# Linear attention and a Mish feed-forward: the attention's small products in plain float32 on parts of TensorE's array

## The chip, the core and the metric

The kernel runs on one core of one Trainium2 chip. The metric is the device time of one execution in microseconds. A token here is one row of the output; the core has TensorE (PE), VectorE (DVE), ScalarE (ACT), GpSimd (POOL) and the queue of SyncE (SP), from which most transfers are started.

## What is computed

```python
kv  = einsum('bhsd,bhse->bhde', k, v)        # 8 batches, 8 heads, 576 rows, 64 columns
out = einsum('bhsd,bhde->bhse', q, kv)
rms = sqrt(mean(out * out, axis=-1) + 1e-6)
x   = (out / rms * g_norm), heads side by side  # 4608 tokens x 512
h   = x @ w_in                                # 512 x 2048
g   = h * tanh(softplus(h))                   # Mish
y   = g @ w_out                               # 2048 x 512, float32
```

The attention has no softmax, so k^T v is a 64 x 64 matrix for each head, and it is small beside the two dense products.

## The kernel before

The 4608 tokens are nine token tiles of 512 (`T`), numbered j = 0 to 8. A batch has 576 rows, so most token tiles hold two segments, the end of batch j - 1 and the beginning of batch j (`segments(j)`): 64 and 448 columns in tile 1, 128 and 384 in tile 2, and so on to 512 alone in tile 8.

**The dense products.** Float32 operands are split into a high part (`nc.scalar.copy` into float32r, line 122) and the rest (`nc.vector.tensor_sub`, line 123). A product is then three float32r matmuls: low times high, high times low, high times high. Both dense products also use a seven-product form of the 2 x 2 block product (forms named A11, S1 and so on, made by `x_form` for the first dense product). One such product is a *slot*: twelve matmuls of 128 x 128 by 256 columns in `mm_in` (line 536). Each token tile has 28 slots (`NS`), so tile j's own products run in slots 28 j to 28 j + 27. The output stage (`mm_out`, line 790) runs after all nine tiles.

**What sets the order.** The order of every engine is written out by hand: `at(slot, f)` puts work behind the product of a slot, `then` puts an eviction ahead of it. Engines and queues take their instructions in that order. The attention of tile j runs in the 28 slots of tile j - 1, and the products k^T v of batch b in those of tile b - 2.

**The attention of a token tile** is done in two units u of four heads, that is, two head pairs a. The steps of a unit, by name:

- `load`, `transpose`: q comes in and is transposed (on DVE from tile 2 on, line 339; on TensorE in tiles 0 and 1).
- `halves`: from tile 2 (`T32`) on, q is split into two float32r parts (lines 122 and 123, tiles fl, fh, fa).
- `project`: x = kv^T q for each head pair and segment. The two 64 x 64 matrices of a pair lie on the diagonal of a 128 x 128 matrix of which the rest is zero. Tiles 0 and 1 use plain float32 (line 369), the others three float32r matmuls (lines 372 to 374).
- `square`, `scaled`: ACT squares the result, DVE scales it by g into the tile x of the dense product.
- `squares`: from tile 2 on, the squares are split as q is.
- `sums`: the squares of each head are added up by a matmul with a 128 x 8 matrix of ones and zeros (`sel`), all eight heads into the same eight partitions of one bank, lines 408 (float32) and 410, 411 (float32r).
- `rstd`, `keep`, `spread`, `normalize`: ACT makes the reciprocal roots, SP stores them to a DRAM tile (line 426) and loads them back on all partitions (line 433), and DVE multiplies x by them (line 441).

**k^T v** of a batch is made in four parts of one head pair each (`k_load`, `k_product`, line 261): four blocks of 128 rows and one of 64, in plain float32, with the even head in PSUM partitions 0 to 63 and the odd head in 64 to 127. Batch 0 has a form of its own on two diagonal 64 x 64 tiles (`kv_first_product`, line 243), which writes the same PSUM bank. `kv_keep` copies the result, splits it (line 285) and places it on the diagonal. The staging tiles of k and v have two buffers.

Of the kernel before, what the change touches and what calls it, by code (L numbers as in the profile page):

```python
# [8 lines left out]
F32 = mybir.dt.float32  # L9
# [18 lines left out]
def linear_attention_rms_mish_ffn(  # L28
# [82 lines left out]
    sel = const.tile([P, NKC, H], F32R, name="sel")  # L111
# [9 lines left out]
    def split(hi, lo, src):  # L121
        nc.scalar.copy(hi, src)  # L122
        nc.vector.tensor_sub(lo, src, hi.bitcast(F32))  # L123
# [102 lines left out]

    kv0 = []

    def kv_first(n):
# [22 lines left out]
    def kv_product(b, h0, nh, km, kr, vm, vr):  # L254
        for i in range(nh // 2):
            for c in range(CM + 1):
                for o in range(2):
                    h = 2 * i + o
                    d = slice(c * D, (c + 1) * D)
                    kt, vt = (km[:, h, d], vm[:, h, d]) if c < CM else (kr[:, h, :], vr[:, h, :])  # L260
                    nc.tensor.matmul(kvps[o * D:(o + 1) * D, b % 2, h0 // 2 + i, :], kt, vt, start=(c == 0), stop=(c == CM))  # L261

    kvf, kvt = [], []

    def kv_tiles():
        for n in range(T32):
            kvf.append(pools["kvf"].tile([P, NKC, P], F32, name=f"kvf{n}"))
            nc.gpsimd.memset(kvf[n], 0.0)  # L270
        for n in range(2):
            kvt.append(kvs.tile([P, 2, NKC, P], F32R, name=f"kv{n}"))
            nc.gpsimd.memset(kvt[n].bitcast(F32), 0.0)

    def kv_keep(b, n):
        for r in (slice(0, D), slice(D, P)):
            if b < T32:
                nc.scalar.copy(kvf[b][r, n, r], kvps[r, b % 2, n, :])
        if b < T32 - 1:
            return  # L280
        t = kvt[b % 2]
        for r in (slice(0, D), slice(D, P)):
            nc.scalar.copy(t[r, 0, n, r], kvps[r, b % 2, n, :])
        for r in (slice(0, D), slice(D, P)):
            nc.vector.tensor_sub(t[r, 1, n, r], kvps[r, b % 2, n, :], t[r, 0, n, r].bitcast(F32))


    def segments(j):
# [18 lines left out]
    qs, ss = {}, {}  # L307

    def unit_steps(j, u):
        st = {}  # L310

        def load():


            t = qs[u] = att.tile([P, 2, T // R * D], F32, name="qs")
            for i in (0, 2, 1, 3):
                for b, s0, cols in segments(j):
                    run = (cols.stop - cols.start) // R * D
                    src = q[b, 4 * u + i // 2, s0:s0 + 1, R * (i % 2):]
                    src = bass.AP(src.tensor, src.offset, [[run, R], [2 * S * D, 2], [1, run - R]])  # L320
# [25 lines left out]
            else:  # L346
                nc.scalar.copy(t, st["ps"])

        def parts(t):
            hi = att.tile([P, 2, T], F32R, name="fh")  # L350
            lo = att.tile([P, 2, T], F32R, name="fa")
            split(hi, lo, t)
            return hi, lo

        def halves():
            if j >= T32:
                st["qh"], st["ql"] = parts(st["q"])

        def project():
            if j == 0 and u == 1:  # L360
                st["x"] = [bank_new("bc").rearrange("p m t -> p (m t)") for _ in range(2)]
            else:
                x2 = st["x2"] = ps_t.tile([P, 2, T], F32, name="x2")
                st["x"] = [x2[:, a] for a in range(2)]
            for a in range(2):
                ps, hp = st["x"][a], 2 * u + a
                for b, _, c in segments(j):
                    if j < T32:
                        nc.tensor.matmul(ps[:, c], kvf[b][:, hp, :], st["q"][:, a, c], start=True, stop=True)
                        continue  # L370
                    kh, kl, qh, ql = kvt[b % 2][:, 0, hp, :], kvt[b % 2][:, 1, hp, :], st["qh"][:, a, c], st["ql"][:, a, c]
                    nc.tensor.matmul(ps[:, c], kl, qh, start=True, stop=False)  # L372
                    nc.tensor.matmul(ps[:, c], kh, ql, start=False, stop=False)  # L373
                    nc.tensor.matmul(ps[:, c], kh, qh, start=False, stop=True)  # L374

        def square():
            st["s"] = att.tile([P, 2, T], F32, name="fl" if j >= T32 else "fh" if j == 0 and u else "fa")
            if "x2" in st:
                nc.scalar.square(st["s"], st["x2"])
            else:  # L380
                for a in range(2):
                    nc.scalar.square(st["s"][:, a], st["x"][a])
# [5 lines left out]
            else:  # L388
                nc.vector.tensor_scalar(o, st["x2"], gcol, None, ALU.mult)

        def squares():
            if j >= T32:
                st["sh"], st["sl"] = parts(st["s"])

        def sums():
            if j == 0:
                st["ss"] = []
                for a in range(2):
                    ps = bank_new("a").rearrange("p m t -> p (m t)") if u == 0 else ps_t.tile([P, T], F32, name="ss") if a == 0 else kvps.rearrange("p b n d -> p (b n d)")
                    nc.tensor.matmul(ps, ones, st["s"][:, a], start=True, stop=True)  # L400
                    st["ss"].append(ps)
                return
            if u == 0:
                ss[j] = ps_t.tile([H, T], F32, name="ss")
            for a in range(2):
                e = sel[:, 2 * u + a, :]
                if j < T32:
                    nc.tensor.matmul(ss[j], e.bitcast(F32), st["s"][:, a], start=u == a == 0, stop=u == a == 1)
                else:
                    nc.tensor.matmul(ss[j], e, st["sl"][:, a], start=u == a == 0, stop=False)  # L410
                    nc.tensor.matmul(ss[j], e, st["sh"][:, a], start=False, stop=u == a == 1)

        def rstd():
            if j == 0:
                r = st["r"] = st["s"]
                for a in range(2):
                    nc.scalar.activation(r[:, a], st["ss"][a], AF.Ln, bias=eps, scale=1.0 / D)
                nc.scalar.activation(r, r, AF.Exp, scale=-0.5)
                return
            r = st["r"] = att.tile([H, T], F32, name="fa" if j < T32 else "fl")  # L420
            nc.scalar.preload_act_table_set("natural_log_exp_and_others")  # L421
            nc.scalar.activation(r, ss[j], AF.Ln, bias=eps[0:H], scale=1.0 / D)
            nc.scalar.activation(r, r, AF.Exp, scale=-0.5)

        def keep():
            nc.sync.dma_start(rd[j], st["r"])

        def spread():

# [10 lines left out]
            else:  # L440
                nc.vector.tensor_mul(o, o, st["rr"])

        return {f.__name__: f for f in (load, transpose, turned, halves, project, square, scaled, squares, sums, rstd, keep, spread, normalize)}


    x = fp.tile([P, NKC, T], F32, name="gf")
# [122 lines left out]
        for s in steps:  # L569
            units[j][u][s]()  # L570

    open_pools(wst, ("w64", 1), ("wd", 1), ("kvf", 1))

    def w64_room():
        return pools["w64"].tile([P, 4, 2 * P, 2], U32, name="w64")
# [35 lines left out]
    weights(2, LOAD)  # L611
    weights(3, LOAD)
    make_identity(nc, ident)
    kv_tiles()
# [4 lines left out]
    nc.gpsimd.memset(sel.bitcast(F32), 0.0)  # L619
    for hp in range(NKC):  # L620
        for o in range(2):
            nc.gpsimd.memset(sel[o * D:(o + 1) * D, hp, 2 * hp + o:2 * hp + o + 1].bitcast(F32), 1.0)

    weights(0, SCALE, JOIN, DIFF)
    do(0, 0, "transpose", "turned")
# [40 lines left out]
    at(5, lambda: kv_keep(1, slice(0, NKC)))  # L666
    for b in range(2, B):
        t = NS * (b - 2)
        loads = (5, 6, 14, 16) if b == 2 else (20 - NS, 22 - NS, 4, 6) if b == 3 else (8 - NS, 10 - NS, 4, 6)
        for p in range(4):  # L670
            at(t + loads[p], lambda b=b, p=p: k_load(b, p))
            at(t + ((12, 14, 16, 18) if b == 2 else (2, 4, 6, 8))[p], lambda b=b, p=p: k_product(b, p))
        at(t + (20 if b == 2 else 11), lambda b=b: kv_keep(b, slice(0, NKC)))

    def attention(j):

        def spread():
# [3 lines left out]
        t = NS * (j - 1)  # L681
        steps = (
            (0, 2, "transpose"), (0, 3, "turned"), (0, 6, "project", "square", "scaled"), (1, 8, "transpose"),
            (1, 9, "turned"), (0, 9, "sums"), (1, 11, "project", "square", "scaled"), (1, 15, "sums"),
        ) if j == 1 else (
            (0, 8 - NS if j > 2 else 9 - NS, "load"), (0, 20 - NS, "transpose"), (1, 22 - NS, "load"), (0, 25 - NS, "halves"),
            (0, 0, "project"), (0, 3, "square", "scaled"), (0, 4, "squares"), (1, 5, "transpose"), (0, 6, "sums"),
            (1, 8, "halves"), (1, 10, "project"), (1, 12, "square", "scaled"), (1, 13, "squares"), (1, 15, "sums"),
        )
        for u, n, *names in steps + ((1, 16, "rstd"), (1, 18, "keep"), (0, 19, "spread0"), (0, 23, "normalize"), (1, 24, "normalize")):  # L690
            at(t + n, lambda u=u, names=names: do(j, u, *names))
# [304 lines left out]
```

## Time and profile before

| what | value |
|---|---|
| median of 3 runs | 871.11 us (870.78 to 873.40) |
| profiled execution: span from first to last instruction | 867.2 us |
| granted TensorE clock, mean | 0.990 |
| TensorE busy | 829.2 us, 96% of the span |
| DVE busy | 604.5 us, 70% |
| ACT busy | 462.4 us, 53% |
| POOL busy | 102.5 us, 12% |
| HBM traffic | 106.89 MB read, 56.49 MB written |

The profile is of one execution. Its page gives the span, and no time for what lies around it, so the span stands beside the runs: these are 3.6 to 6.2 us longer. Lines such as L261 are lines of the kernel file before. "PE" is matmul work and "PEld" the loading of stationary operands. Matmuls are pipelined, so the records of neighbours overlap: what a group costs is read from the start of its first record to the start of the next group. A plain float32 matmul of the program stands as two records. Names in `out<-in` are the program's tiles without buffer numbers: `x` is the projection's PSUM tile, `s` that of k^T v, `a` and `bc` the PSUM banks of the dense product, `gf` its operands' forms, `ss` the sums.

### The profile page before, as it was taken

Reading aid. Unit: us, or ns where it says so; the run is one execution under the profiler, and the core shown is the slowest. Engines: PE = TensorE matmul, PEld = TensorE weight load, DVE = VectorE, ACT = ScalarE, POOL = GpSimd, SP = SyncE. Lnnn points to the kernel's source line nnn. Section 1 sums busy time; section 2 is a strip of 40 time slices with the busy share of each in tenths; the row PEclk is TensorE's granted clock in tenths of the full one; section 3 lists DMA queues with packets and bytes.
Section 4 is the critical chain, followed back from the end, with each engine's and each line's share of the span. In section 5 each row is a group of like instructions: output and inputs, shape, how many; then the busy total and the mean of one; then the engine's idle time right before and its main releaser. Section 6 shows DMA issues by size and latency. Waiting matters only on the chain.

```text
span 867.2 us, 17267 instructions
## 1 busy us (share of the span) xinstructions
PE 829.2 (96%) x7036; PEld 799.0 (92%) x7036; DVE 604.5 (70%) x778; ACT 462.4 (53%) x681; POOL 102.5 (12%) x173
## 2 busy tenths in 40 slices
PE   4868999999999999999999999999999999999997
PEld 3656999999999999999899999999999999999997
DVE  4788676757766576677765788767767777776772
ACT  3666656655566656566666654444443344334441
POOL 2000122232222313112122100000000000000000
PEclk9889999999999999999999999999999999999999
DMA  9975686878877674757376972543444444344421
GB/s 277 258 230 150 202 261 229 282 240 276 249 234 224 217 228 168 239 182 271 128 233 239 383 260 78 179 145 114 134 131 122 122 122 122 122 125 147 148 69 49
DMA packets 121007, 164.52 MB, mean 190 GB/s; under 512 B 25184, under 2 KB 96096, under 8 KB 120672
## 3 DMA queue, kind: packets, MB, share of 16 engines
q1 hardware_dynamic: 107328, 116.42, 44.5%
q0 software_dynamic: 13504, 46.93, 14.4%
q8 instruction: 55, 0.90, 0.5%
q14 instruction: 24, 0.20, 0.1%
q10 hardware_dynamic: 96, 0.07, 0.0%
HBM read 106.89 MB, written 56.49 MB: 188 GB/s over the span
## 4 chain that ended last, share of the span: by engine, by line
PE 76%; ACT 9%; DVE 8%; issue 3%; DMA 2%; SPq 2%; ACTq 0%; DVEq 0%
PE a L790 22%; PE a L536 18%; PE bc L790 16%; PE bc L536 14%; PE s L261 2%; DVE gf L123 1%; ACT wf L122 1%; ACT gf L122 1%; SPq L304 1%; PE x L373 1%; ACT L421 1%; PE x L374 1%; DVE ur L557 1%; PE x L372 1%; DVE wf L123 1%
## 5 line engine op out<-in xcount | busy, mean ns | idle before, releaser
L790 PE MATMUL a<-wf,gf 128*128 128x256 f32 x1632 | 201.8, 283 | 0.5 <-DVE ur L835 0.5
L790 PEld LDWEIGHTS a<-wf,gf 128*128 128x128 f32 x1632 | 198.4, 192 | 0.7 <-DVE ur L835 0.7
L123 DVE TENSOR_TENSOR gf<-g,gf 128x1024 fp32r<-128x1024 f32 (+1 forms) x123 | 132.9, 1087 | 87.1 <-ACT gf L122 87.1
L536 PE MATMUL a<-gf,wf 128*128 128x256 f32 x1296 | 172.5, 286 | 6.9 <-ACT ur L513 6.6
L536 PE MATMUL bc<-gf,wf 128*128 128x256 f32 x1296 | 172.5, 286 | 2.1 <-ACT gf L122 1.9
L536 PEld LDWEIGHTS a<-gf,wf 128*128 128x128 f32 x1296 | 162.7, 192 | 12.3 <-ACT ur L513 8.3
L536 PEld LDWEIGHTS bc<-gf,wf 128*128 128x128 f32 x1296 | 163.3, 193 | 3.7 <-ACT gf L122 2.0
L122 ACT CAST gf<-g 128x1024 fp32r<-128x1024 f32 (+1 forms) x123 | 114.6, 939 | 90.7 <-DVE g L770 65.7
L790 PE MATMUL bc<-wf,gf 128*128 128x256 f32 x1224 | 152.7, 283 | 0.9 <-DVE gf L123 0.9
L790 PEld LDWEIGHTS bc<-wf,gf 128*128 128x128 f32 x1224 | 149.4, 192 | 1.3 <-ACT gf L122 0.7
L119 ACT ACTIVATE ur<-ur 128x1024 f32<-128x1024 f32 x36 | 38.1, 1059 | 54.7 <-DVE ur L557 54.7
L536 PE MATMUL a<-a,wf 128*128 128x256 f32 x432 | 58.8, 286 | 5.2 <-DVE ur L557 5.2
L536 PEld LDWEIGHTS a<-a,wf 128*128 128x128 f32 x432 | 55.1, 192 | 8.2 <-DVE ur L557 6.6
L123 DVE TENSOR_TENSOR fa<-fl,fh 128x1024 fp32r<-128x1024 f32 x28 | 34.2, 1221 | 18.1 <-ACT fh L122 16.9
L122 ACT CAST gf<-a 128x1024 fp32r<-128x1024 f32 x17 | 17.9, 1051 | 53.4 <-DVE a L767 50.9
L123 DVE TENSOR_TENSOR gf<-gf 128x512 fp32r<-128x512 f32 x45 | 30.2, 690 | 23.1 <-ACT gf L122 23.1
L513 ACT COPY ur<-a 128x512 f32<-128x512 f32 (+1 forms) x53 | 27.4, 517 | 32.2 <-PE a L790 24.6
L560 POOL DMA_DIRECT2D gd<-ula x36 | 26.1, 725 | 146.3 <-ACT ula L119 104.6
L122 ACT CAST gf<-gf 128x512 fp32r<-128x512 f32 x45 | 26.9, 618 | 30.1 <-DVE gf L460 17.5
L557 DVE TENSOR_TENSOR ula<-bc,ula 128x512 f32<-128x512 f32 x36 | 24.7, 686 | 23.8 <-PE bc L536 23.6
L504 ACT COPY ur<-bc 128x512 f32<-128x512 f32 (+1 forms) x53 | 27.5, 518 | 24.5 <-PE bc L790 23.0
L555 POOL DMA_DIRECT2D gd<-ulb x36 | 25.6, 711 | 94.7 <-ACT ulb L119 87.7
(147 smaller groups left out, 944.8 us busy)
## 6 DMA issues: line engine op xcount, KB each, us to landing
g<-gd SPq DMA_DIRECT2D x18, 2048.0 KB, 8.6
gd<-ur POOLq DMA_DIRECT2D x36, 512.0 KB, 5.1
gd<-ula POOLq DMA_DIRECT2D x36, 256.0 KB, 4.4
gd<-ulb POOLq DMA_DIRECT2D x36, 256.0 KB, 4.8
w<-in_moe_w_out_dram SPq DMA_DIRECT2D x32, 256.0 KB, 5.3
km<-in_k_dram SPq DMA_DIRECT2D x28, 256.0 KB, 4.4
vm<-in_v_dram SPq DMA_DIRECT2D x28, 256.0 KB, 4.9
wf<-wod SPq DMA_DIRECT2D x6, 896.0 KB, 8.0
```

The costliest lines, as they stand in the source:

```text
L119: nc.scalar.activation(o, i, AF.Mish)
L122: nc.scalar.copy(hi, src)
L123: nc.vector.tensor_sub(lo, src, hi.bitcast(F32))
L261: nc.tensor.matmul(kvps[o * D:(o + 1) * D, b % 2, h0 // 2 + i, :], kt, vt, start=(c == 0), stop=(c == CM))
L304: nc.sync.dma_start(rows[j][t0 - c * P:t1 - c * P, c, h0 * D:(h0 + n) * D].rearrange("p (h d) -> p h d", d=D), src)
L504: then(t + 2, lambda: nc.scalar.copy(dst(st, "22"), st["c"]))
L513: then(t + 4, lambda: nc.scalar.copy(dst(st, "12"), st["a"]))
L536: nc.tensor.matmul(bank[:, jj], w[:, right, a, kc, :], xf[:, b, kc, :], start=first and jj == kc == s == 0, stop=(kc == 1 and s == 2), ski ...
L555: at(t + 2, lambda: eng.dma_start(left[:, :, TH:T], o))
L557: nc.vector.tensor_add(o, bank, o)
L560: at(t + 3, lambda: eng.dma_start(left[:, :, 0:TH], o))
L790: nc.tensor.matmul(bank, gf[:, a, c, :], wo[c][:, :, right, b, :], start=first and c == s == 0, stop=(c == NF2 - 1 and s == 2), skip_group ...
```

## The change

All of the attention's products are plain float32 now, and each is placed on a part of the array.

- `halves`, `squares` and the split of k^T v are gone, and with them the zero-filled matrices. `kv_keep` copies a batch's matrices once, as they lie in PSUM.
- `project` issues a 64 x 64 matmul for each head of a pair instead of a 128 x 128 one for the pair. From tile 2 on, the second pair of a unit is *turned*: its q comes in with the heads exchanged, k^T v with its halves exchanged, so the four heads of a unit use four different 64 x 64 tiles of the array. Tiles 0 and 1 aren't turned, so both pairs use the two diagonal tiles. Batch 1 is needed both ways, so DVE also copies it exchanged (`kvx`).
- `sums` is done once for a tile from tile 1 on, in slot 15, as four 128 x 32 products: head pair hp goes to the column strip of partitions 32 hp to 32 hp + 31. `keep` stores two rows of each strip, four transfers instead of one.
- The plan of k^T v moves: two parts go behind the same slot, from batch 3 on two in slot 0 and two in slot 10, where the projections also are, and their loads go out earlier relative to them.

```diff
+    def half(o, turned=False):
+        o = 1 - o if turned else o
+        return slice(o * D, (o + 1) * D)
...
-                    nc.tensor.matmul(kvps[o * D:(o + 1) * D, b % 2, h0 // 2 + i, :], kt, vt, start=(c == 0), stop=(c == CM))
+                    hp = h0 // 2 + i
+                    nc.tensor.matmul(kvps[half(o, b >= T32 and hp % 2), b % 2, hp, :], kt, vt, start=(c == 0), stop=(c == CM))
...
+    kvt = [kvs.tile([P, NKC, D], F32, name=f"kv{n}") for n in range(2)]
+    kvx = kvs.tile([P, 2, D], F32, name="kvx")
     def kv_keep(b, n):
...
+        nc.scalar.copy(kvt[b % 2][:, n], kvps[:, b % 2, n, :])
+        if b == T32 - 1:
+            for o in range(2):
+                nc.vector.tensor_copy(kvx[half(o, True)], kvps[half(o), b % 2, 1::2, :])
...
-        def halves():
-            if j >= T32:
-                st["qh"], st["ql"] = parts(st["q"])
...
-            for a in range(2):
-                ps, hp = st["x"][a], 2 * u + a
-                for b, _, c in segments(j):
...
-                    nc.tensor.matmul(ps[:, c], kl, qh, start=True, stop=False)
-                    nc.tensor.matmul(ps[:, c], kh, ql, start=False, stop=False)
-                    nc.tensor.matmul(ps[:, c], kh, qh, start=False, stop=True)
+            for b, _, c in segments(j):
+                for a in range(2):
+                    hp, turned = 2 * u + a, j >= T32 and a == 1
+                    kv = kvx[:, u] if turned and b < T32 else kvt[b % 2][:, hp]
+                    for o in range(2):
+                        r = half(o, turned)
+                        nc.tensor.matmul(st["x"][a][half(o), c], kv[r], st["q"][r, a, c], start=True, stop=True)
...
-                    nc.tensor.matmul(ss[j], e, st["sl"][:, a], start=u == a == 0, stop=False)
-                    nc.tensor.matmul(ss[j], e, st["sh"][:, a], start=False, stop=u == a == 1)
+            ss[j] = ps_t.tile([P, T], F32, name="ss")
+            for n in range(2):
+                for a in range(2):
+                    hp = 2 * n + a
+                    nc.tensor.matmul(ss[j][hp * R:(hp + 1) * R], sel, sq[j, n][:, a], start=True, stop=True)
...
-            nc.sync.dma_start(rd[j], st["r"])
+            for n in range(NKC):
+                nc.sync.dma_start(rd[j][2 * n:2 * n + 2], st["r"][n * R:n * R + 2])
...
-        loads = (5, 6, 14, 16) if b == 2 else (20 - NS, 22 - NS, 4, 6) if b == 3 else (8 - NS, 10 - NS, 4, 6)
+        loads = (5, 6, 14, 15) if b == 2 else (19 - NS, 20 - NS, 1, 2) if b == 3 else (11 - NS, 12 - NS, 1, 2)
...
-            at(t + ((12, 14, 16, 18) if b == 2 else (2, 4, 6, 8))[p], lambda b=b, p=p: k_product(b, p))
+            at(t + ((12, 13, 18, 18) if b == 2 else (0, 0, 10, 10))[p], lambda b=b, p=p: k_product(b, p))
```

How the order moves on TensorE, at the beginning of the slots in which tile 4's attention runs. The names with a number are single buffers: `x2` is the projection's PSUM tile, `kv0` and `kv1` the kept k^T v of two batches, `s2` the PSUM tile of k^T v. Before, from the second half of the first projection on:

```order
L372 MATMUL x2_2435<-fh_2379,kv1_175 128x256
L373 MATMUL x2_2435<-fa_2380,kv1_175 128x256
L374 MATMUL x2_2435<-fh_2379,kv1_175 128x256
L372 MATMUL x2_2435<-fh_2379,kv0_173 128x256
L373 MATMUL x2_2435<-fa_2380,kv0_173 128x256
L374 MATMUL x2_2435<-fh_2379,kv0_173 128x256
L536 MATMUL bc_2451<-gf_342,wf0_210 128x256 x6
L536 MATMUL bc_2451<-gf_342,wf1_281 128x256 x6
L536 MATMUL a_2287<-a22_482,wf6_764 128x256 x6
L536 MATMUL a_2287<-a22_482,wf7_850 128x256 x6
L261 MATMUL s2_123<-vm_2022,km_2020 64x64 x8
L261 MATMUL s2_123<-vr_2023,kr_2021 64x64 x2
```

The same place now:

```order
L510 MATMUL a<-gf,wf_196 128x256 x6
L510 MATMUL a<-gf,wf_268 128x256 x6
L267 MATMUL s_123<-vm,km 64x64 x8
L267 MATMUL s_123<-vr,kr 64x64 x2
L267 MATMUL s_123<-vm,km 64x64 x8
L267 MATMUL s_123<-vr,kr 64x64 x2
L354 MATMUL x_2387<-fl,kv_125 64x256 x4
L354 MATMUL x_2387<-fl,kv_124 64x256 x4
L510 MATMUL bc<-gf,wf_196 128x256 x6
```

Two k^T v products that stood two slots apart stand together ahead of the projection, and the projection's twelve matmuls became eight.

On SP's queue, around the store of tile 3's reciprocal roots, before (`rd3` is the DRAM tile, `qs` the next q, `w64` a block of w_out):

```order
L322 DMA qs_2032<-in_q_dram 32x2x480 x8
L138 DMA w64_2044<-in_moe_w_out_dram 128x2x256 x2
L222 DMA km_2076<-in_k_dram 128x2x256
L223 DMA kr_2077<-in_k_dram 64x2x64
L222 DMA vm_2078<-in_v_dram 128x2x256
L223 DMA vr_2079<-in_v_dram 64x2x64
L426 DMA rd3_115<-fl_2211 8x512
L433 DMA fh_2258<-rd3_115 64x2x512 x2
L433 DMA fa_2261<-rd3_115 64x2x512 x2
```

and now:

```order
L315 DMA qs_1947<-in_q_dram 32x2x480 x8
L138 DMA w64_1959<-in_moe_w_out_dram 128x2x256 x2
L222 DMA km_2036<-in_k_dram 128x2x256
L223 DMA kr_2037<-in_k_dram 64x2x64
L222 DMA vm_2038<-in_v_dram 128x2x256
L223 DMA vr_2039<-in_v_dram 64x2x64
L222 DMA km_2057<-in_k_dram 128x2x256
L223 DMA kr_2058<-in_k_dram 64x2x64
L222 DMA vm_2059<-in_v_dram 128x2x256
L223 DMA vr_2060<-in_v_dram 64x2x64
L400 DMA rd3_115<-fl_2144 2x512 x4
L407 DMA fh_2194<-rd3_115 64x2x512 x2
```

The store became four transfers, and both loads for the next batch's first two products stand ahead of it.

More of the change, by code (lines that the diff above doesn't have):

```diff
@@ L110, in linear_attention_rms_mish_ffn @@
     ones = const.tile([P, P], F32, name="ones")
-    sel = const.tile([P, NKC, H], F32R, name="sel")
+    sel = const.tile([P, R], F32, name="sel")
     gd = [tc.dram_tile([P, NFC, T], F32, name=f"gd{i}") for i in range(NT)]
@@ L306, in linear_attention_rms_mish_ffn @@
     rows = {}
-    qs, ss = {}, {}
+    qs, ss, sq = {}, {}, {}
     def unit_steps(j, u):
@@ L441, in normalize @@
                 nc.vector.tensor_mul(o, o, st["rr"])
-        return {f.__name__: f for f in (load, transpose, turned, halves, project, square, scaled, squares, sums, rstd, keep, spread, normalize)}
+        return {f.__name__: f for f in (load, transpose, turned, project, square, scaled, sums, rstd, keep, spread, normalize)}
     x = fp.tile([P, NKC, T], F32, name="gf")
@@ L618, in linear_attention_rms_mish_ffn @@
     nc.gpsimd.memset(ones[D:P, D:P], 1.0)
[L619 to L622, printed above, removed]
+    nc.gpsimd.memset(sel, 0.0)
+    for o in range(2):
+        nc.gpsimd.memset(sel[o * D:(o + 1) * D, o:o + 1], 1.0)
     weights(0, SCALE, JOIN, DIFF)
```

57 lines of the change are left out of this document (10 added, 47 removed).

## The prediction

> **What bounds the kernel now.** I read the page's engine shares first, then busy time by stretch, then what TensorE waits for in the long middle stretch, then TensorE's own timeline in one token tile.
>
> ```profile
> PE 829.2 (96%) x7036; PEld 799.0 (92%) x7036; DVE 604.5 (70%) x778; ACT 462.4 (53%) x681; POOL 102.5 (12%) x173
> ```
>
> ```profile
> 0.00:40.00 40.00, 24.90 (x241) 17.68 (x242) 22.80 (x31) 20.84 (x31) 5.98 (x25) 0.94 1.01 282
> 40.00:100.00 60.00, 48.86 (x396) 41.37 (x397) 49.84 (x71) 40.08 (x58) 4.77 (x7) 0.93 0.56 169
> 100.00:440.00 340.00, 336.32 (x2935) 321.94 (x2933) 235.36 (x344) 212.50 (x320) 78.45 (x121) 1.00 0.71 228
> ```
>
> The columns are PE, weight loads, DVE, ACT, POOL, granted clock, DMA share and GB/s. From 100 to 440 us TensorE is busy for 336.3 of 340 us at the full clock, while DVE is busy for 235 and ACT for 213. There, what TensorE is spared comes off the end, and what DVE and ACT are spared does not. Before 100 us TensorE has gaps. The output stage after 440 us is untouched.
>
> ```profile
> PE a L536 <- DVE ur L557: 3.5, 2, 1.8
> PE a L536 <- ACT ur L513: 3.3, 2, 3.2
> ```
>
> ```profile
> L536 PE MATMUL a<-gf,wf 128*128 128x256 f32 x984 | 129.2, 284 | 2.6 <-ACT ur L513 2.6
> L410 PE MATMUL ss<-fa,sel 128*8 128x512 f32 x28 | 11.1, 396 | 1.0 <-DVE fa L123 1.0
> ```
>
> The first two rows are TensorE's largest waits from 40 to 100 us. The other two are groups from 100 to 440, with the idle time ahead of them as the last figure: 2.6 us for an eviction by ACT, and 1.0 us for the split of the squares.
>
> TensorE's timeline in token tile 4:
>
> ```profile
> 210.53 0.28 PE L372 MATMUL x<-fh,kv 128*128 128x256 f32 x1
> ...
> 211.97 1.60 PE L536 MATMUL bc<-gf,wf 128*128 128x256 f32 x12
> 213.41 1.60 PE L536 MATMUL a<-a,wf 128*128 128x256 f32 x12
> 214.94 0.69 PE L261 MATMUL s<-vm,km 128*64 128x64 f32 x16
> 215.55 0.33 PE L261 MATMUL s<-vr,kr 64*64 64x64 f32 x4
> 215.81 1.69 PE L536 MATMUL a<-gf,wf 128*128 128x256 f32 x12
> 217.34 1.60 PE L536 MATMUL bc<-gf,wf 128*128 128x256 f32 x12
> ...
> 222.80 0.69 PE L261 MATMUL s<-vm,km 128*64 128x64 f32 x16
> 223.42 0.33 PE L261 MATMUL s<-vr,kr 64*64 64x64 f32 x4
> 223.68 0.40 PE L410 MATMUL ss<-fa,sel 128*8 128x512 f32 x1
> ...
> 224.62 0.65 PE L536 MATMUL a<-gf,wf 128*128 128x256 f32 x4
> ```
>
> I take differences of starts, since ends overlap. A slot's twelve products take 1.44 us (211.97 to 213.41). A projection takes 1.44. A k^T v product takes 0.87, but the slots on both sides of it take 1.53, so it costs 0.87 + 2 x 0.09 = 1.05. The sums take 0.94 behind a product whose leaving price they contain, so I count 0.9.
>
> **Two prices that the change rests on.** First, plain float32 on one tile, and what it costs to enter and leave it:
>
> ```profile
> 69.57 1.88 PE L408 MATMUL ss<-fa,sel 128*8 128x512 f32 x4
> 71.38 1.69 PE L536 MATMUL a<-gf,wf 128*128 128x256 f32 x12
> 72.91 1.60 PE L536 MATMUL bc<-gf,wf 128*128 128x256 f32 x12
> ```
>
> ```profile
> L408 PE MATMUL ss<-fa,sel 128*8 128x512 f32 x8 | 3.8, 593 | 0.0
> ```
>
> Line 408 issues two products of 512 columns, and four records stand there: float32 runs as two passes. Their pitch is (1.88 - 0.59) / 3 = 0.43 us, or 54 ns for 64 columns. The block takes 69.57 to 71.38, 1.81 us; the slot behind it is 0.09 too long, and I add as much ahead. That makes 1.99 = 4 x 0.43 + 0.27, so 0.27 is what such a block pays beside its passes.
>
> Second, tiles at once. The product rows above hold 16 passes of 64 columns in two column tiles: 16 x 54 ns is 0.86 us in a row, and they take 0.61. Four more passes take 0.26 with all entering and leaving. The first batch uses two diagonal tiles, which write the same PSUM bank:
>
> ```profile
> 21.51 2.31 PE L243 MATMUL s<-wf,wf 64*64 64x64 f32 x72 [0.60 <-DMA wf<-in_v_dram]
> ```
>
> 72 passes in a row would be 3.9 us; 2.31 / 72 is 32 ns a pass, tail included, so two tiles work at once. The trace has pairs by columns and pairs on the diagonal; four at once, two row halves writing the same PSUM partitions (in other banks), and four column strips it has not. For a projection of 512 columns the bounds are therefore two passes' time (0.86 us, four at once) and eight (3.44, one at once), with two at once at 1.72. I take 0.86 for both: the four projection tiles ask of each row half what the two column tiles of L261 do, two streams. The strips are less sure, with four streams on all rows.
>
> The Trainium skill, TensorEngine Tiling (Array Packing), under Gotcha 1: PSUM Pressure, says that different row tiles cannot access one PSUM bank at the same time. By that rule a projection's two tiles of one head pair, which write one bank, could not overlap. The diagonal row above disagrees: both its tiles write one bank, and a pass takes 32 ns rather than 54.
>
> **The change part by part.**
>
> *Token tiles 2 to 6 (five).* Now each has four products, two projections and two sums: 4 x 1.05 + 2 x 1.6 + 2 x 0.9 = 9.2 us. The 1.6 is the middle of the split projections' range, by these rows (448 + 64 columns: 1.81; one segment: 1.39):
>
> ```profile
> 358.90 0.37 PE L372 MATMUL x<-fh,kv 128*128 128x448 f32 x1
> ...
> 360.71 1.56 PE L536 MATMUL bc<-gf,wf 128*128 128x256 f32 x11
> ...
> 406.58 0.40 PE L372 MATMUL x<-fh,kv 128*128 128x512 f32 x1
> ...
> 407.97 1.60 PE L536 MATMUL bc<-gf,wf 128*128 128x256 f32 x12
> ```
>
> Then, there are two float32 blocks of two products and a projection: 2 x (0.61 + 0.26) + 0.86 + 0.1 for the change of tile shape + 0.18 for entering and leaving = 2.9; and one block of sums, 0.86 + 0.27 = 1.13. That is 6.9, say 7.0. Saved: 2.2 x 5 = 11.0 us.
>
> *Tiles 7 and 8* have no products left. Tile 7: 2 x 1.81 + 1.8 + half of the 1.0 us wait for the split, 5.9, becomes 3 x 1.13 = 3.4: saved 2.5. Tile 8: 2 x 1.39 + 1.8 + 0.5 = 5.1 becomes 3.4: saved 1.7.
>
> *Tile 1* already uses float32. Its projections aren't turned, so both head pairs lie on the same two tiles: four pass times, as now, nothing saved. Its two sums blocks, 4.0 us, become one of 1.13: 2.85 on TensorE, but in the stretch with gaps. The bounds are 0 and 2.85; I take the middle, 1.5. Tile 0's projections also remain four pass times: 0. Two products of the second batch share a block: 0.2.
>
> *DVE and ACT.*
>
> ```profile
> L123 DVE TENSOR_TENSOR fa<-fl,fh 128x1024 fp32r<-128x1024 f32 x28 | 34.2, 1221 | 18.1 <-ACT fh L122 16.9
> L122 ACT CAST fh<-fl 128x1024 fp32r<-128x1024 f32 x28 | 29.4, 1051 | 0.0
> ```
>
> These 56 instructions go, 34 us of DVE and 29 of ACT, beside smaller copies of k^T v. They lie under TensorE's work and are worth only what shortens its 2.6 us of waiting for ACT: 0 to 2.6, and I take 0.6, since an eviction also waits for its own product. The reciprocal roots run on 128 partitions instead of 8, with the same 512 elements in each: 0.
>
> *SP.* One store of the roots becomes four.
>
> ```profile
> L426 SPq DMA_DIRECT2D rd<-fl x7: 281/311/316, 144.5 to 438.4; - x7
> ...
> DVE gf L441 <- DMA fa<-rd: 11.7, 8, 2.2
> ...
> PE x L334 <- DMA wf<-in_q_dram: 7.0, 1, 7.0
> ```
>
> Three more issues of 0.31 us make the spread 0.9 us later, and DVE's normalize already waits for it. Behind it on DVE stand the input forms of the next tile, due four to five slots later (1.44 us each), and a split of 1.2 us no longer stands between them. Bounds 0 and 8 x 0.9 = 7.5; I take 0. The q loads keep their count. The k and v loads go out eight or nine slots ahead of their second products, where now they go two ahead: no DMA wait appears. POOL loses memsets at the start, when TensorE waits for q anyway: 0.
>
> Sum: 11.0 + 2.5 + 1.7 + 1.5 + 0.2 + 0.6 = 17.5 us. The profiled span of 867.2 becomes 849.7. The runs are 3.6 to 6.2 us above that span, and nothing here touches this rest, so the median goes from 871.1 to 853.6.
>
> **The rivals.**
> 1. *Strips go two at a time.* Eight sums blocks (tiles 1 to 8) cost 0.86 more each: 6.9, so 860.5. For it: no row has four streams over all rows. Against: two streams show no loss.
> 2. *The projection goes two at a time* because row halves that share output partitions queue: 14 x 0.86 = 12.0, so 865.6; with rival 1 too, 872.5, no change. For it: no row of such a pair. Against: diagonal and column pairs overlap fully.
> 3. *Slower: TensorE starts a tile's second pass before it looks at the next tile.* Four tiles then take five pass times instead of two, 3 x 0.43 more for each of the 8 sums blocks, and 4.5 in a projection of two half segments, 1.1 more for each of 14: 25.7, so 879.3. It decides above 0.86 + 17.5 / 22 = 1.66 us a block. Against: four passes of 64 columns (215.55) leave after 0.26, and the 72 keep 32 ns.
> 4. *The bank rule holds* though L243 speaks against it: a projection goes two at a time (12.0), and tiles 0 and 1 lose their pairs, 4 x 1.72 = 6.9: 872.5. The page is the one named above.
> 5. *New waits give back half*: blocks of 2.9 us pile evictions, or the later spread stalls the next tile: 4 to 8 us, so about 860.
>
> **How the numbers follow.** All four at once, 853.6 with its own range 849 to 858: 0.60. Rival 1: 0.13. Rival 2 alone: 0.07, with rival 1: 0.06. Rival 3: 0.04. Rival 4: 0.02. Rival 5: 0.08. The range from 848 to 866 holds the first, rivals 1, 2 alone and 5, 0.88, less for unknown sizes at its edges. About 0.3% (2.6 us) is what a measurement of this kernel can tell from no change. Faster: 0.87. Same: 0.08, the cases at 872.5. Slower: 0.05.
>
> **What would show it.** In the changed trace: projections with four starts within some tens of ns and about 0.86 us for their passes (1.72 is rival 2, over 1.9 rival 3); sums blocks of about 0.95 us to the next slot's start (1.8 is rival 1); the span from 100 us to the output stage some 15 us shorter; no DMA wait on TensorE there. What makes it wrong is tiles that overlap less, or evictions that arrive late behind the long blocks.

## The result, and the profile after

| | before | after |
|---|---|---|
| median | 871.46 us (870.78 to 873.40, 4 runs) | 851.48 us (851.22 to 852.39, 4 runs) |
| span of the profiled execution | 867.2 us | 849.2 us |

The ratio is 0.978, with an interval from 0.976 to 0.979. The prediction was 853.6 us, faster. The span fell by 18.0 us and the median by 20.0. Runs of the kernel before that stood beside the experiments had medians of 870.0 to 871.4 us, single ones from 868.5, so the profiled execution of before is one of its quicker ones; what makes its executions differ was not traced. Each of those runs lies 1.7 to 1.8 us above its own span, and the runs of the kernel after lie 1.9 to 2.0 above theirs. So the 3.6 to 6.2 us that the prediction took for a rest which nothing touches are that small rest and a difference between executions. The forecast went out from the span of 867.2 and put the new one at 849.7, against 849.2; the 2.0 us by which the median moved further are nearly all of what it missed.

The engine shares of the kernel after, and its busy time by stretch in the columns of before (PE, weight loads, DVE, ACT, POOL, clock, DMA share, GB/s):

```profile
PE 811.5 (96%) x7112; PEld 776.4 (91%) x7112; DVE 566.5 (67%) x738; ACT 432.8 (51%) x642; POOL 99.5 (12%) x163
```

```profile
0.00:40.00 40.00, 25.27 (x268) 17.39 (x268) 23.75 (x32) 20.15 (x29) 2.71 (x15) 1.00 0.98 279
40.00:100.00 60.00, 46.79 (x393) 40.17 (x394) 47.74 (x68) 39.63 (x56) 4.78 (x7) 0.86 0.57 177
100.00:440.00 340.00, 338.42 (x3128) 319.32 (x3127) 210.24 (x323) 194.44 (x304) 83.23 (x128) 1.00 0.77 244
```

TensorE is busy 338.4 of 340 us in the middle stretch, as before: it bounds both kernels there, and does more of the dense product in the same time. The stretch from 40 to 100 us still has the gaps that it had. TensorE's two largest waits on other engines from 40 to 100 us (total, count, longest; its wait for loads of v there is 4.5 us, 2.9 before), and then the groups of 100 to 440 us, with idle time ahead last:

```profile
PE a L510 <- DVE ur L531: 4.6, 2, 2.9
PE a L510 <- ACT ur L487: 4.4, 1, 4.4
```

```profile
L510 PE MATMUL a<-gf,wf 128*128 128x256 f32 x1055 | 136.7, 283 | 0.2 <-ACT ur L487 0.2
L510 PE MATMUL a<-a,wf 128*128 128x256 f32 x360 | 49.1, 286 | 1.4 <-DVE ur L531 1.3
L384 PE MATMUL ss<-fa,sel 128*32 128x512 f32 x28 | 7.4, 605 | 0.0
```

The 2.6 us for an ACT eviction and the 1.0 us for the split of the squares are gone. Two waits for DVE, 1.3 us, are new. TensorE's timeline in the attention of token tile 4, at the place that the prediction showed, then the sums of the same tile, then the first projection of 448 + 64 columns (start, duration):

```profile
206.67 0.69 PE L267 MATMUL s<-vm,km 128*64 128x64 f32 x16
207.29 0.33 PE L267 MATMUL s<-vr,kr 64*64 64x64 f32 x4
207.55 0.69 PE L267 MATMUL s<-vm,km 128*64 128x64 f32 x16
208.16 0.27 PE L267 MATMUL s<-vr,kr 64*64 64x64 f32 x2
208.18 0.43 PE L354 MATMUL x<-fl,kv 64*64 64x256 f32 x2
208.27 0.23 PE L267 MATMUL s<-vr,kr 64*64 64x64 f32 x2
208.33 1.03 PE L354 MATMUL x<-fl,kv 64*64 64x256 f32 x14
209.29 1.70 PE L510 MATMUL bc<-gf,wf 128*128 128x256 f32 x12
...
233.88 0.62 PE L384 MATMUL ss<-fa,sel 128*32 128x512 f32 x2
233.90 0.62 PE L384 MATMUL ss<-fh,sel 128*32 128x512 f32 x2
234.34 0.60 PE L384 MATMUL ss<-fa,sel 128*32 128x512 f32 x2
234.35 0.60 PE L384 MATMUL ss<-fh,sel 128*32 128x512 f32 x2
234.88 1.70 PE L510 MATMUL a<-a,wf 128*128 128x256 f32 x12
...
348.01 1.10 PE L354 MATMUL x<-fl,kv 64*64 64x448 f32 x16
349.04 1.69 PE L510 MATMUL bc<-gf,wf 128*128 128x256 f32 x12
```

The block of two products and a projection stands from 206.67 to 209.29, 2.62 us; with what the two neighbouring slots are too long it costs 2.81 (the term was 2.9). In the sums the four strips make their first passes from 233.88 to 233.90 and their second 0.45 us later: four at once, and 1.00 us to the next slot's start. The projection takes 1.03, two pass times and the change of shape.

To see where TensorE's time goes I took differences of its starts in token tiles 1 to 7, which hold the attention of tiles 2 to 8. A slot without attention lasts 1.44 us; what it lasts longer is waiting. What slots with attention last longer is the price of the attention blocks; where such a slot is longer than its like in the other tiles, the excess counts as waiting. The two columns hold to about half a microsecond. The kernel before, beside which each was timed, had medians of 870.0 (1 to 4), 871.4 (6 to 9) and 870.3 us (5, 10 to 12), so differences of medians across these groups are good to about 1.5 us.

| token tiles 1 to 7, us | waiting | blocks | median, us | ratio to before (interval) |
|---|---|---|---|---|
| before | 5.0 | 57.7 | 871.46 | |
| after | 3.6 | 41.3 | 851.48 | 0.978 (0.976 to 0.979) |
| 1 not turned | 2.5 | 53.2 | 861.07 | 0.990 (0.988 to 0.992) |
| 2 sums in one strip | 3.1 | 59.2 | 867.93 | 0.997 (0.996 to 0.998) |
| 3 k^T v spread as before | 0.9 | 46.7 | 853.69 | 0.981 (0.979 to 0.983) |
| 4 splits put back | 20.4 | 41.3 | 867.46 | 0.998 (0.997 to 0.999) |
| 5 as 4, DVE's half alone | 18.2 | 41.6 | 863.92 | 0.993 (0.991 to 0.995) |
| 6 3 and 4 together | 9.3 | 47.3 | 863.96 | 0.991 (0.990 to 0.993) |
| 7 before, without splits | 1.2 | 57.5 | 864.41 | 0.992 (0.990 to 0.993) |
| 8 before, with the new plan | 7.9 | 56.9 | 872.68 | 1.002 (1.000 to 1.003) |
| 9 tile 1's sums as before | | | 850.69 | 0.976 (0.975 to 0.978) |
| 10 eight stores | 5.4 | 41.3 | 855.33 | 0.983 (0.981 to 0.984) |
| 11 small blocks first | 2.8 | 39.8 | 849.38 | 0.976 (0.975 to 0.977) |
| 12 11, batch 3 spread | 1.0 | 41.2 | 848.24 | 0.975 (0.973 to 0.976) |

Before to after, the blocks give 16.4 us and the waits 1.4, together 17.8 of the span's 18.0.

### The profile page after: what moved, and what is told of

Same layout as the page of the kernel before. It is cut to its first block, busy times and chain, and to the rows that moved or that the text cites. A ratio compares the mean times of both kernels' runs of the same rounds, so it can differ in the third digit from the quotient of the medians.

```text
span 849.2 us, 17322 instructions
## 1 busy us (share of the span) xinstructions
PE 811.5 (96%) x7112; PEld 776.4 (91%) x7112; DVE 566.5 (67%) x738; ACT 432.8 (51%) x642; POOL 99.5 (12%) x163
## 4 chain that ended last, share of the span: by engine, by line
PE 81%; DVE 8%; ACT 4%; DMA 3%; SPq 2%; issue 1%; DVEq 0%; ACTq 0%
PE a L762 22%; PE a L510 21%; PE bc L762 17%; PE bc L510 16%; PE s L267 2%; PE x L354 1%; DMA vm<-in_v_dram 1%; DVE gf L123 1%; ACT gf L122 1%; ACT wf L122 1%; SPq L297 1%; DVE fl L149 1%; DVE fl L150 1%; DVE wf L123 1%; PE ss L384 1%
## 5 line engine op out<-in xcount | busy, mean ns | idle before, releaser
L510 PE MATMUL a<-a,wf 128*128 128x256 f32 x432 | 60.7, 291 | 7.9 <-DVE ur L531 7.9
L122 ACT CAST gf<-a 128x1024 fp32r<-128x1024 f32 x17 | 17.9, 1051 | 53.4 <-DVE a L739 50.9
L119 ACT ACTIVATE ula<-ula 128x512 f32<-128x512 f32 x36 | 22.7, 632 | 22.0 <-DVE ula L531 22.0
```

The source lines that it names most:

```text
L119: nc.scalar.activation(o, i, AF.Mish)
L510: nc.tensor.matmul(bank[:, jj], w[:, right, a, kc, :], xf[:, b, kc, :], start=first and jj == kc == s == 0, stop=(kc == 1 and s == 2), ski ...
```

## The experiments

Each is an edit of the kernel after, except 7 and 8.

**1. Not turned.** Both head pairs of a unit on the two diagonal tiles, in all token tiles.

```diff
-                    hp, turned = 2 * u + a, j >= T32 and a == 1
+                    hp, turned = 2 * u + a, False
```

> The changed kernel with the turn taken out: q comes in with its heads in order, k^T v isn't exchanged, so from tile 2 on both head pairs of a unit use the two diagonal 64x64 tiles. Everything else as changed. Theory A (the gain of the projections is that four tiles of the array work at once): each of the 14 projections of tiles 2 to 8 takes four pass times instead of two, 0.86 us more, 12.0 us in all, so about 863.5. Theory B (the gain comes from the freed DVE and ACT and from the moved plan, and two tiles would do): within 2 us of the changed kernel's 851.5.

Measured: 861.07 us, 9.6 more than after, 2.4 less than theory A. The same projection as above, from its timeline:

```profile
354.96 1.95 PE L354 MATMUL x<-fl,kv 64*64 64x448 f32 x16
356.84 1.70 PE L510 MATMUL bc<-gf,wf 128*128 128x256 f32 x12
```

It takes 1.88 us to the next start against 1.03, so 0.85 us, a pair of passes, comes back for each of the 14 projections; the blocks cost 11.9 us more, and 1.1 us of waiting goes. All four tiles work at once in the kernel after, among them the pair of one head pair that writes one PSUM bank. This is rival 2's mechanism, made to happen, at the price that it had.

**2. Sums in one strip.** All four head pairs add up in the first strip, one behind the other.

```diff
-                    nc.tensor.matmul(ss[j][hp * R:(hp + 1) * R], sel, sq[j, n][:, a], start=True, stop=True)
+                    nc.tensor.matmul(ss[j][0:R], sel[:, hp], sq[j, n][:, a], start=hp == 0, stop=hp == 3)
```

> The changed kernel with all four products of the sums in one column strip: the matrix of ones has a place for each head pair, and the four add up in the first 32 partitions. Theory A (four strips at once): a block of sums takes eight pass times instead of two, 6 x 0.43 = 2.6 us more; seven blocks of tiles 2 to 8 give 18.0 us, and tile 1's block lies where TensorE waits anyway, so 869 to 872. Theory B (strips don't work at once, or the end does not hang on them): within 2 us of 851.5.

Measured: 867.93 us, 16.5 more. The block in its timeline:

```profile
238.45 1.90 PE L384 MATMUL ss<-fa,sel 128*32 128x512 f32 x4
240.19 1.88 PE L384 MATMUL ss<-fh,sel 128*32 128x512 f32 x4
242.00 1.70 PE L510 MATMUL a<-a,wf 128*128 128x256 f32 x12
```

It takes 3.55 us instead of 1.00. With its neighbours' share that is 3.74 against 1.18, 2.56 in each of seven tiles: 17.9, less 0.5 of waiting. The profiled spans differ by 17.3 us. The median is 1 us below the expected range, whose low end already gave tile 1's block nothing; half of that is the waiting, and the rest is within what medians across groups can tell. Without the strips nearly the whole gain is lost.

**3. k^T v spread as before.** The loads and products of all batches stand where they stood.

```diff
-        loads = (5, 6, 14, 15) if b == 2 else (19 - NS, 20 - NS, 1, 2) if b == 3 else (11 - NS, 12 - NS, 1, 2)
+        loads = (5, 6, 14, 16) if b == 2 else (20 - NS, 22 - NS, 4, 6) if b == 3 else (8 - NS, 10 - NS, 4, 6)
...
-            at(t + ((12, 13, 18, 18) if b == 2 else (0, 0, 10, 10))[p], lambda b=b, p=p: k_product(b, p))
+            at(t + ((12, 14, 16, 18) if b == 2 else (2, 4, 6, 8))[p], lambda b=b, p=p: k_product(b, p))
```

> The changed kernel with the plan of k^T v before: loads and products in the slots that they had, each product by itself. Theory A (a float32 block pays for entering and leaving): in tiles 2 to 6 four products of 1.05 and two projections of 1.2 us make 6.6 us in place of two blocks of 2.81, 1.0 us more a tile, 5.0 in all, so about 856.5, and no new wait. Theory B (the plan was moved because the loads would come late): TensorE waits for k or v at the old places and the time goes up by more than 8 us. Theory C (the place is worth nothing): 851.5.

Measured: 853.69 us, 2.2 more. The blocks cost 5.4 us more, 1.0 to 1.1 in each of five tiles, as the terms have it; but 2.7 us of waiting goes. So half of what the joined blocks spare comes back as waits, a small form of rival 5.

**4. Splits put back.** The 56 split instructions return to their places and inputs, and nothing reads their result, so the wait of TensorE's blocks on them is left out. They share one result buffer, which the splits before did not.

```diff
+        def parts(t):
+            nc.scalar.copy(dummy, t)
+            nc.vector.tensor_sub(dummy, t, dummy.bitcast(F32))
...
+            (0, 25 - NS, "halves"), ... (0, 4, "squares"), ... (1, 8, "halves"), ... (1, 13, "squares"),
```

> The changed kernel with the 28 casts on ACT and the 28 subtractions on DVE put back in the slots that they had, on q and on the squares, with results that nothing reads. Theory A (they lay under TensorE's work): 851.5 to 853.5, the 1 to 2 us that TensorE waits less for evictions. Theory B (the freed DVE and ACT are what made it faster): 8 us or more is lost.

Measured: 867.46 us, 16.0 more: the splits' term of 0.6 is not what they cost the changed kernel. TensorE's largest waits on other engines from 100 to 440 us:

```profile
PE a L521 <- DVE ur L542: 6.2, 5, 2.4
PE a L521 <- ACT ur L498: 5.7, 8, 1.2
```

The timeline of both kernels at the same place of token tile 2, DVE's rows and TensorE's, first with the splits, then the kernel after:

```profile
171.96 1.28 DVE L381 TENSOR_SCALAR gf<-x,gcol 128x1024 f32<-128x1024 f32 x1 [0.23 <-ACT fa L371]
173.38 1.23 DVE L351 TENSOR_TENSOR dummy<-fa,dummy 128x1024 fp32r<-128x1024 f32 x1
174.53 0.68 DVE L542 TENSOR_TENSOR ula<-bc,ula 128x512 f32<-128x512 f32 x1
...
178.64 0.68 DVE L542 TENSOR_TENSOR ur<-a,ur 128x512 f32<-128x512 f32 x1
...
179.38 1.69 PE L521 MATMUL a<-a,wf 128*128 128x256 f32 x12 [2.35 <-DVE ur L542]
```

```profile
167.11 1.28 DVE L370 TENSOR_SCALAR gf<-x,gcol 128x1024 f32<-128x1024 f32 x1 [0.24 <-ACT fa L360]
168.31 0.68 DVE L531 TENSOR_TENSOR ula<-bc,ula 128x512 f32<-128x512 f32 x1
...
172.42 0.68 DVE L531 TENSOR_TENSOR ur<-a,ur 128x512 f32<-128x512 f32 x1
...
173.16 1.69 PE L510 MATMUL a<-a,wf 128*128 128x256 f32 x12 [0.34 <-DVE ur L531]
```

From the scaling to the end of the addition on `ur`, which frees a PSUM bank, DVE takes 7.36 us with the split and 5.99 without it. TensorE, which writes that bank next, waits 2.35 us instead of 0.34. DVE has slack on average (232 of 340 us busy with the splits), but its queue in these slots has next to none: it is busy 7.15 of the 7.36 us, and 5.92 of the 5.99. The waits sit in token tiles 1, 2, 6 and 7 and hardly in 3 to 5; which other work of DVE makes that difference was not tried.

**5. DVE's half alone.** As 4, without ACT's 28 copies; `nc.vector.tensor_sub(dummy, t, t)` remains.

> The changed kernel with DVE's half of the splits alone put back: 28 subtractions of 128 x 1024 in the old slots, which need nothing of ACT. Both halves had cost 16.0 us. Theory A (DVE's queue is what comes late): 10 us or more of it returns, 861 or more. Theory B (ACT's casts ahead of its evictions, and the hand-over between the two, make most of it): less than 6 us returns, below 857.5.

Measured: 863.92 us, 12.4 more than after. DVE's half returns three quarters of the 16.0, so DVE's queue is the main place, and the rest comes with ACT's copies. Since DVE alone writes the shared buffer here, that buffer is not the reason for the larger part. The profiled execution, which gave the table's row, was the longest of the four (866.62 us), so its 18.2 us of waiting is high for the median.

**6. Splits back on the old plan**: the edits of 3 and 4 together.

> The changed kernel with both put back: the 28 casts and 28 subtractions (results that nothing reads) and the old plan of k^T v. The splits alone had cost 16.0 us (867.5), the old plan alone 2.2 (853.7). Theory A (the splits hurt because, with two k^T v products gone from slots 1 to 9, DVE's and ACT's queue there is longer than TensorE's time, so the evictions come late): the products between the slots give that time back, and the splits cost less than 5 us on top of the old plan, so 854 to 859. Theory B (the splits hurt wherever TensorE stands, since DVE's and ACT's total is the next limit): the costs add, 868 to 870.

Measured: 863.96 us, 10.3 more than 3, between the two forecasts. With the old plan the splits cost less (10.3) than with the new one (16.0), but far more than their term: about half of what they cost the changed kernel, or more, does not hang on where k^T v stands. The traces say where. From 110 to 210 us (about tiles 1 and 2) TensorE waits 7.0 us for DVE and ACT in experiment 4 and 1.4 here, so there the spread products give the cover back, as theory A has it. From 355 to 450 us (tiles 6 and 7, which have no k^T v products to spread) it waits 4.8 us in both.

**7. The kernel before without its splits.** The projection reads slices of a w_in tile, and the sums read the squares twice, in place of the parts. It leaves the parts out, so it does not compute the function; only its time is of use. TensorE also waits neither for q nor for a split there.

```diff
-                st["qh"], st["ql"] = parts(st["q"])
+                st["qh"] = st["ql"] = wf[0][:, 0:2].rearrange("p f s m n -> p f (s m n)")
...
-                st["sh"], st["sl"] = parts(st["s"])
+                st["sh"] = st["sl"] = st["s"]
```

> The kernel before with its 56 split instructions of q and the squares left out and all of TensorE's work kept: the projection reads two slices of the first w_in tile in place of the parts of q, and the sums read the squares twice, which ACT writes as float32r. The splits themselves are left out of the computation. Theory A (in the kernel before, the splits lay under TensorE's work): 867 to 870, at most the 3.6 us that TensorE idled from 100 to 440 us. Theory B (freed DVE and ACT alone are the gain): below 862.

Measured: 864.41 us, 7.0 less than the 871.43 beside it, between the forecasts. Its waiting in token tiles 1 to 7 falls from 5.0 to 1.2, 3.8 us; the other half is no longer than the gap between the profiled execution of before and its median, and I don't place it. Even beside the old TensorE work the splits were not free.

**8. The kernel before with the new plan of k^T v** (its loads and products by the numbers of the kernel after).

> The kernel before with the plan of k^T v alone moved, two products behind slot 0 and two behind slot 10. Theory A (a block's entering and leaving is worth 0.18 us for each product that is joined, but DVE and ACT with their splits no longer keep up in slots 1 to 9): slower than before by 2 to 8 us, 872 to 878. Theory B (only entering and leaving counts): 2 x 5 x 0.18 = 1.8 us faster, about 868.

Measured: 872.68 us, 1.2 more than the kernel before (interval 0.3 to 2.8 us). The plan alone is worth nothing there: the blocks cost 0.8 less, the waits 2.9 more.

**9. Tile 1's sums as before**, in two blocks with a 128 x 8 matrix for each head pair, in slots 9 and 15 (`(0, 9, "sums")` beside `(1, 15, "sums")`), and one store.

> The changed kernel with tile 1's sums as before: two blocks of two products into the same eight partitions, in slots 9 and 15, 4.0 us of TensorE in place of 1.2. Theory A (in the first 100 us TensorE waits for evictions, so what it is spared there is waited for instead): within 1.2 us of 851.5. Theory B (the prediction's term): 1.5 to 2.8 us slower, 853 to 854.3.

Measured: 850.69 us, 0.8 less than after (single runs 850.1 to 851.7, against 851.2 to 852.4). The 2.85 us that TensorE is spared in tile 1 were worth nothing that shows. In the kernel after, TensorE waits 2.87 us for DVE behind the block of sums; in the kernel before, 1.77 behind the second of its two.

**10. Eight stores** of the roots, one row each, instead of four of two rows.

```diff
+                for o in range(2):
+                    nc.sync.dma_start(rd[j][2 * n + o:2 * n + o + 1], st["r"][n * R + o:n * R + o + 1])
```

> The changed kernel with eight stores of one row instead of four stores of two for the reciprocal roots, about 1.0 us more on SP's queue in each of eight tiles, and so a later spread and normalize. Theory A (DVE has the time): 851.5, with some 8 us more of DVE waiting for the loads. Theory B (the chain sets the next tile's start): up to 8 us slower.

Measured: 855.33 us, 3.9 more. DVE's waits for the spread roots, total, count and longest, first in the kernel after, then with eight stores:

```profile
DVE gf L415 <- DMA fh<-rd: 13.5, 7, 4.3
DVE gf L415 <- DMA fa<-rd: 10.4, 7, 2.4
```

```profile
DVE gf L416 <- DMA fh<-rd: 16.1, 7, 5.3
DVE gf L416 <- DMA fa<-rd: 12.6, 8, 3.0
```

DVE waits 28.7 instead of 23.9 us, and TensorE 1.8 us more in tiles 1 to 7. The cover of this path is thin: four more issues break it. The other 2 us lie in the trace ahead of tile 1 and behind tile 7, about 1 us in each, and are not explained. What four stores cost over one was not isolated.

**11. Small blocks first.** In the first product of a pair, the block of 64 rows comes ahead of the four blocks of 128 rows, so that the 128-row blocks of both products stand together.

```diff
+            cs = [CM, *range(CM)] if h0 // 2 % 2 == 0 and b > T32 else range(CM + 1)
```

> The changed kernel with the blocks of the first of two joined k^T v products in another order from batch 3 on: the 64-row block ahead of the four 128-row blocks, so that the two products' 128-row blocks stand side by side and one change of tile shape less is paid in each of ten blocks. Theory A (a change of tile shape costs 0.1 to 0.15 us): 1.0 to 1.5 us faster than the changed kernel, about 850. Theory B (it costs nothing): 851.5.

Measured: 849.38 us, 2.1 less than after. The block, from the timeline of TensorE:

```profile
205.42 0.33 PE L268 MATMUL s<-vr,kr 64*64 64x64 f32 x4
205.69 1.15 PE L268 MATMUL s<-vm,km 128*64 128x64 f32 x32
206.77 0.27 PE L268 MATMUL s<-vr,kr 64*64 64x64 f32 x2
...
207.90 1.70 PE L511 MATMUL bc<-gf,wf 128*128 128x256 f32 x12
```

It lasts 2.48 instead of 2.62 us. The order before was 128 rows, 64, 128, 64 and the projection on tiles of the last shape; now it is 64, 128, 64. That is one change of tile shape fewer, for 0.14 us.

**12. And batch 3's products spread** over four slots, as before the change, since the kernel after waits most in tile 1 (2.2 of its 3.6 us), where they stand.

```diff
+... (20 - NS, 22 - NS, 4, 6) if b == 3 ...
+... (2, 4, 6, 8) if b == 3 else (0, 0, 10, 10) ...
```

> The kernel with the 64-row block first, and batch 3's four products in their old slots 2, 4, 6, 8, since tile 1 is the one with the longest waits for evictions (2.2 us against 0.4 with the old plan, for blocks that cost 1.1 more). Theory A: 0.7 us faster than with the 64-row block first alone, about 849.3. Theory B (tile 1's waits aren't set by the place of the products): up to 1 us slower than it.

Measured: 848.24 us (848.07 to 848.64), 3.2 less than after, 1.1 less than experiment 11, and the fastest median of all. The waits fall from 2.8 to 1.0 us; the blocks cost 1.4 more. By the traces that is 0.4 us, and the runs of 11 (848.5 to 850.6) overlap with these, so how much the spread adds is not settled.

## Why the prediction was right, step by step

- **Four tiles at once, and blocks by passes: right.** A tile's attention was put at 9.2 us before and 7.0 after for tiles 2 to 6; it measures 9.23 on average and 6.81. Tile 7 gave 2.7 (predicted 2.5), tile 8 gave 1.7 (1.7). The three terms, 11.0 + 2.5 + 1.7 = 15.2 us in the prediction, came to 16.4. Rivals 1 to 4 are excluded: 1 by the four starts within 20 ns and experiment 2, 2 and 4 by experiment 1, 3 by projections of 1.03 us. The bank rule of the Trainium skill (TensorEngine Tiling (Array Packing), Gotcha 1: PSUM Pressure) does not hold for these tiles: the eight matmuls of a projection (16 records), of which each head pair shares a bank, take 1.03 us, the time of four tiles at once.
- **Tile 1: wrong.** The middle of 0 and 2.85 was taken, 1.5; undoing it gains 0.8 us, so no worth is seen. Here, where the engine has gaps, the lower bound was the one to take. The 0.2 for batch 2 lies in the same stretch and does not show.
- **The splits: the mis-sized term.** Of 17.8 us, only 1.4 came as less waiting, near the 0.6. But the bound, 0 to 2.6, was wrong. It counted one group's idle time in the kernel before; all of TensorE's waiting there is 5.0. And it took the cover of the old TensorE work, while the same change shortens that work: the splits are worth 7.0 us alone (experiment 7), and 16.0 in the changed kernel (4). The sum priced both parts as done together, with TensorE's work shorter and the splits gone, which is what the kernel after is. That it hit so closely is in part luck: the blocks gave 1.2 us more than said, the waits 0.8 more, and tile 1 and batch 2 1.7 less.

The four corners, with the old plan of k^T v throughout, show it. The row of new work is the change on TensorE, in the stores and in tile 1 together. The corners with the splits are not quite alike: TensorE waits for the parts in the kernel before, and does not in 6.

| us | with the splits | without | what the splits cost |
|---|---|---|---|
| old TensorE work | 871.46 (before) | 864.41 (7) | 7.0 |
| new TensorE work | 863.96 (6) | 853.69 (3) | 10.3 |
| what the work gives | 7.5 | 10.7 | |

Without the splits' removal the shorter products would have given 7.5 of some 18 us; the plan then adds 2.2 with the splits gone (3 against after), and takes 3.5 with them (6 against 4). The 10.3 is a difference across groups, so it is hardly apart from the 7.0. The traces' sums of waiting and blocks in tiles 1 to 7 give the same order: the splits cost 4.0 us beside the old work (before against 7), 9.0 beside the new work on the old plan (6 against 3) and 16.8 on the new plan (4 against after).

- **The stores: 0 held, with a thin margin** (experiment 10). Neither normalize nor a DMA wait holds TensorE in the middle stretch.
- **The plan: right on the blocks** (1.0 to 1.1 us a tile), and without the waits that it brings, 2.7 us. No DMA wait appears from 100 to 440 us, as said. Not all loads go out earlier relative to their products: from batch 4 on those of the first two parts went from 22 slots ahead to 17 and 16, those of the last two from 2 to 9 and 8.

## What to carry to other kernels

Small float32 products of one engine's critical path are worth packing on as many tiles of the array as the operands allow, with the shapes grouped. A cost hidden beside the bounding engine has to be priced again at that engine's new pace: the same 56 instructions cost about 7, 10 or 16 us by what they lay beside. An average of 68% busy (DVE, experiment 4) did not say that the queue had room in the slots where its work stood.

## What the runs showed of the hardware

Plain float32 matmuls on four 128 x 32 strips, all reading all 128 rows, run fully at once: 1.00 us for the block of sums, against 3.55 in one strip (experiment 2). No row of the kernel before had shown four streams over all rows.

A free tile may start ahead of earlier instructions. In the kernel after, the two records of each matmul, its passes, need not stand together: two passes of the projection start at 208.18, ahead of the last two of k^T v at 208.27, although these come first in the program. In the attention of token tile 2 a whole matmul is overtaken. The program has two on `kv` ahead of the first on `kvx`, each with two passes; the timeline has one pass on `kv`, then the first on `kvx`, and the others behind:

```profile
110.61 0.32 PE L354 MATMUL x<-fl,kv 64*64 64x128 f32 x1
110.62 0.32 PE L354 MATMUL x<-fl,kvx 64*64 64x128 f32 x1
110.70 0.22 PE L267 MATMUL s<-vr,kr 64*64 64x64 f32 x2
110.75 0.27 PE L354 MATMUL x<-fl,kvx 64*64 64x128 f32 x1
110.76 0.28 PE L354 MATMUL x<-fl,kv 64*64 64x128 f32 x2
```

By the program, the last k^T v products lie on rows 0 to 63, and the first two passes can be those whose tiles, on rows 64 to 127, are free. The Trainium skill, TensorE: Matmul & The Clock Gate, Part 3: Packing small matmuls, states that matmuls start and end in program order; for matmuls on different tiles this trace shows otherwise in the starts.

The clock can be low behind a wait. In the kernel after, both projections of tile 1 have the same size. TensorE's timeline, and the granted clock (the last but two of the columns) in the stretch of each:

```profile
54.88 2.93 PE L510 MATMUL a<-gf,wf 128*128 128x256 f32 x12 [4.42 <-ACT ur L487]
57.75 3.17 PE L354 MATMUL x<-fh,kv 64*64 64x64 f32 x16
60.85 1.69 PE L510 MATMUL a<-gf,wf 128*128 128x256 f32 x12
...
72.80 1.95 PE L354 MATMUL x<-fh,kv 64*64 64x64 f32 x16
74.68 1.58 PE L510 MATMUL bc<-gf,wf 128*128 128x256 f32 x11
```

```profile
56.00:62.00 6.00, 6.00 (x34) 3.86 (x34) 5.82 (x10) 2.95 (x6) 0.00 (x0) 0.64 0.66 190
72.00:76.00 4.00, 4.00 (x35) 2.69 (x34) 2.90 (x4) 4.00 (x7) 0.72 (x1) 1.00 0.19 70
```

Behind a wait of 4.42 us the first takes 3.10 us at a mean clock of 0.64, the second 1.88 at 1.00. In the stretch with gaps a wait can thus cost more than its own length. It need not: the k^T v product behind a wait of 1.98 us for v, at 47.90, takes 0.88 us, at a clock of 1.00, as in the middle stretch.
